# One block and a more detailed timing simulator for the instruction order of a two-layer attention and Mish kernel

## The chip, the cores and the metric

One core of one Trainium2 chip. The metric is the device time of one execution in microseconds (us), as the median of several runs. The core has a matrix engine (TensorE, "PE" in the profile; its weight loads are listed as "PEld"), a vector engine (VectorE, DVE), an activation engine (ScalarE, ACT), a general engine (GpSimd, POOL) and a queue engine (SyncE, SP). Each engine takes its own instructions in the order in which they stand in the program. In this kernel every DMA is issued by SP.

## The reference

Two layers of the same pair of blocks, with the same weights, on x of 2048 rows by 640 columns in float32 (the heads' reshapes are left out):

```
for _ in range(2):
    n = layernorm(x)
    q, k, v = split(n @ wqkv)                 # 32 heads of 20
    pq, pk = q @ w_phi, k @ w_phi             # per head
    phi_q = [softmax(pq), softmax(-pq)]       # 40 features per head
    phi_k = [softmax(pk), softmax(-pk)]
    kv, z = phi_k^T v, sum over rows of phi_k
    x = x + ((phi_q kv) / (phi_q z + 1e-6)) @ wo
    n = layernorm(x)
    x = x + mish(n @ w1 + b1) @ w2            # 640 -> 1536 -> 640
```

## The kernel before

**Precision.** Every product of two activations or weights in the projections and dense layers is made from a high and a low half of each operand: three matmuls (high·high, low·high, high·low). The high half is an ACT copy to a rounded type (`r1h`, `r2h`, `xth`), the low half a subtraction (`r1l`, `r2l`, `xtl`) on DVE or POOL. Weights are split in `split` (L139 to L146): a DMA into a stage `st`, an ACT copy (L145), a subtraction (L146).

**Stages of a layer.** The main loop stands in L1016 to L1043 and calls three functions per layer.

- `attend_first` (L492) goes through 8 blocks of 256 rows, each of two tiles of 128 rows. For each tile it makes a query, a key and a value tile: `project` (L424) runs 30 matmuls of 128 x 320 columns for one. `features` (L459) makes the two softmaxes: ACT copies from PSUM and takes the exponential; DVE reduces (L467, L476) and takes the reciprocal (L477); POOL multiplies (L478) and, for queries, subtracts (L468). For a key tile, 22 small matmuls (L543) add phi_k^T v into two PSUM tiles. Query features are stored to DRAM in `e_d` (L552). Row statistics come from `norm_stats` (L275, L277, DVE) and `norm_scale` (L284, L285 on POOL, L287 on DVE).
- Layer 0 has a start of its own: the query and key weights are loaded raw (L239), centered (L247, L248 on DVE, L249 on ACT), and folded with w_phi on PE (`fold_phi`, L261), then split on ACT and DVE (L266, L267). The value weights come by `load_v_weights` through stages named `st` and `v` (DMA L144). L305 transposes normalized rows, L313 makes their low halves. L514 and L518 store a transposed copy of x.
- `finish_kv` (L621) masks and transposes the accumulated kv (L626 DVE, L633 PE) into `kvb`. It lies inside the turn from `attend_first` to `attend_second`.
- `attend_second` (L640) goes through the blocks again. `load(b)` brings the two `e` tiles back (L650). `features_t` transposes them on PE (L664) and evicts by DVE (L668) or ACT (L670); `averages` runs the small matmuls (L685) and divides on DVE (L694 to L698); `output` multiplies by wo (L713) and adds x (L715). At the end of each block `at(b)` loads and splits a part of w1 or w2, and from b=1 on runs the stages of the dense part's layernorm (`NormColumns`: squares L368 on ACT, centering L363 and sums of squares L373 on DVE, sums over features L360 on PE).
- `dense` (L787) goes through 4 groups of 512 rows and 12 tiles of 128 hidden features: 15 matmuls of `hidden` (L804, 128 x 512), Mish (L763 to L785: exponential on ACT, three DVE steps, logarithm and exponential on ACT, three DVE steps, copy L784 on ACT and subtraction L785 on POOL), and 15 matmuls of `contract` (L817). At its end in layer 0 it begins the next layer: `fetch_first` (L855) loads the first 256 rows of the new x from `x2r_d` (L859), a copy that `turn` (L828, L832) stored, and query weights that layer 0 had put away in `wp_d` (L178).

**Buffers.** Four `big` buffers of 128 x 1280 hold `e` tiles and Mish temporaries, two `x` buffers rows, six `ol` buffers pairs, ten `xt` buffers split rows, four `row` buffers small rows. PSUM has two `mm` tiles of two banks and four `one` tiles of one bank.

**What sets the order.** The kernel is written against a tile framework. It traces the instructions, tracks which buffers each reads and writes, chooses the order of the instructions on each engine, and adds the semaphore waits. `dense` contains `with tc.manual_schedule(engines=...)` (L962): for PE, DVE, ACT and POOL, the order inside it is the written one, from a list of due places (`plan`, `do`); SP is not in the set. In the rest of the kernel the framework chooses, save for some hints: `issue_after` (ACT's copies through `act`, L126 to L133, are chained; `features_t` waits for the last `averages`; `at(b)` for a load). A DMA uses one of eight landing semaphores, so SP, before it issues a DMA, also waits for the landing of the one eight before it.

Of the kernel before, what the change touches and what calls it, by code (L numbers as in the profile page):

```python
# [16 lines left out]
P = 128  # L17
S = 2048
D = 640
F = 1536  # L20
H = 32
DH = 20
KD = D // P
# [14 lines left out]
LAYERS = 2  # L38
# [6 lines left out]
def kernel(  # L45
# [13 lines left out]
    nc = tc.nc  # L59
# [17 lines left out]
    def x_tile():  # L77

        return work.tile([P, KD, SB], F32, tag="x", name="xt", bufs=2)
# [7 lines left out]
    def part_tile(name):  # L87

        return work.tile([P, 2, BLK], F32R, tag="xt", name=name, bufs=10)

    def row_tile(width=D, dtype=F32, name="row"):
        return work.tile([P, VW], dtype, tag="row", name=name, bufs=4)[:, :width]
# [4 lines left out]
    def col_block(t, c0, n):  # L97

        return t.rearrange("(k p) s -> p k s", p=P)[:, :, c0:c0 + n]
# [4 lines left out]
    b1s = const.tile([P, KF], F32, name="b1s")  # L104
# [14 lines left out]
    x0_d = dram.tile([D, S], F32, name="x0_d")  # L119
    x1_d = dram.tile([D, S], F32, name="x1_d")  # L120
    x2_d = dram.tile([D, S], F32, name="x2_d")
# [4 lines left out]
    def act(*args, **kw):  # L126

        if last_act[0] is None:
            ins = nc.scalar.activation(*args, **kw)
        else:  # L130
            with tc.issue_after(last_act[0]):
                ins = nc.scalar.activation(*args, **kw)  # L132
        last_act[0] = ins.ins  # L133
# [5 lines left out]
    def split(hi, lo, src, width, eng, stage=None):  # L139
        for c0 in range(0, width, D):  # L140
            c1 = min(width, c0 + D)
            st = row_tile(name="st") if stage is None else stage()
            st = st[:, :c1 - c0]
            nc.sync.dma_start(st, src[:, c0:c1])  # L144
            nc.scalar.activation(hi[:, c0:c1], st, AF.Copy)  # L145
            eng.tensor_tensor(lo[:, c0:c1], st, hi[:, c0:c1].bitcast(F32), op=ALU.subtract)  # L146

    def r1_pair(k):
        return tuple(wts.tile([P, F], F32R, tag=f"r1{s}{k}", name=f"r1{s}{k}") for s in "hl")
# [4 lines left out]
    def r2_pair(j):  # L154
        if j >= 10:
            w = r2_wide(j)
            return w[:, 0], w[:, 1]
        return tuple(wts.tile([P, D], F32R, tag=f"r2{s}{j}", name=f"r2{s}{j}") for s in "hl")
# [62 lines left out]
    def load_w2(fs):  # L221

        ws = {}
        for f in fs:
            ws[f] = r2_pair(f)
            split(ws[f][0], ws[f][1], w2[f * P:(f + 1) * P, :], D, nc.gpsimd)
        return ws
# [188 lines left out]
    def split_chunk(xt, k, into):  # L416

        hi, lo = (part_tile(n).rearrange("p c s -> p (c s)") for n in ("xth", "xtl"))
        act(hi, xt[:, k], AF.Copy)
        nc.vector.tensor_tensor(lo, xt[:, k], hi.bitcast(F32), op=ALU.subtract)  # L420
        into.append((hi, lo))
# [65 lines left out]
    def fetch_super(src, sb):  # L487
        xt = x_tile()
        nc.sync.dma_start(xt, col_block(src, sb * SB, SB))
        return xt  # L490
# [130 lines left out]
    def finish_kv(kva, kvz, mask):  # L621
# [7 lines left out]
        for src, q0, n in ((acc, 0, 4), (acz, 4, 2)):  # L629
# [6 lines left out]
            else:  # L636
                nc.vector.tensor_copy(kvb[:, 4 * P:5 * P], ps[:120, 0])
                nc.vector.tensor_copy(kvb[:80, 5 * P:5 * P + 42], ps[:80, 1, :42])

    def attend_second(x_src, x_dst, acc, at, at_end):  # L640
        kva, kvz, o_ws, advance = acc
        mask = row_tile(name="mask")
# [82 lines left out]
        for b in range(NB):  # L725
            cur = nxt
            if b + 2 < NB:
                gate = load(b + 2)
            xt = fetch_cols(x_src, b, r2_wide(10 + b % 2, F32).rearrange("p s d -> p (s d)"))
            if b + 1 < NB:  # L730
                with tc.issue_after(num[0]):
                    phs = features_t(b + 1)
                if b == 0:
                    cur.all()
                nxt = averages(phs)
            output(cur, xt, 0)
            if b + 1 < NB:
                nxt.all()
            else:
                for k in range(2):  # L740
                    at_end(k)
            output(cur, xt, 1)
            output(cur, xt, 2)
            if b + 1 == NB:
                for k in range(2, KD):
                    at_end(k)
            nc.sync.dma_start(col_block(x_dst, b * BLK, BLK), xt)
            if b + 1 < NB:
                with tc.issue_after(gate.ins):
                    at(b)  # L750
# [262 lines left out]
        rows, xts, q_ws = begun[0]  # L1013
        return rows, xts, kv_ws, q_ws

    first = None  # L1016
    for layer in range(LAYERS):
        last = layer == LAYERS - 1
        acc = attend_first(layer, x, first)
        if layer == 0:  # L1020
            nc.sync.dma_start(b1s, b1)
        w1s = []
        w2s = {}
        x1t = [None, None]

        def at(b):
            if b < KD:
                w1s.append(r1_pair(b))
                split(w1s[b][0], w1s[b][1], w1[b * P:(b + 1) * P, :], F, nc.gpsimd)
            else:  # L1030
                w2s.update(load_w2(((0, 1), (2, 3, 4))[b - KD]))
            if b == 1:
                x1t[0] = fetch_super(x1_d, 0)
                x1t[1] = NormColumns(x1t[0]).stages()
            elif b in (2, 3, 4):
                next(x1t[1])

        def at_end(k):
            split_chunk(x1t[0], k, first)

        first = []
        attend_second(x2_d if layer else x0_d, x1_d, acc, at, at_end)
        first = dense(x1_d, out if last else x2_d, w1s, w2s, first, last)  # L1043


# [36 lines left out]
```

## Time and profile before

| | |
|---|---|
| runs shown | 1509.74, 1512.21, 1507.96 us; median 1509.74 |
| profiled execution | 1507.05 us, span 1505.2 us, mean granted PE clock 0.995 |
| PE busy / share | 1455.5 us, 97% |
| DVE, ACT, POOL busy | 1157.1, 619.6, 486.1 us |
| PE idle before its first matmul | 9.58 us |
| DMA | 167.89 MB, mean 112 GB/s |

The stages lie about so in the span: `attend_first` from 0 to 280 and 770 to 1010 us, `attend_second` from 280 to 405 and 1010 to 1130, `dense` from 405 to 770 and 1130 to 1505.

How to read the views: a timeline row has the start in us, the duration (of a whole run of like instructions, if the count behind the x is over 1), the engine, the line of the kernel, the operation, output<-inputs, shapes, the count, and in brackets the idle time of the engine just before, with what ended it. A row of the view by windows has the window in us and its length, then the busy time of PE, PEld, DVE, ACT and POOL with the number of instructions, the mean granted PE clock (1.0 is full speed), the share of time in which the DMA engines were busy, and what they moved in GB/s.

### The profile page before, as it was taken

How to read it: one execution, taken by the hardware profiler on the slowest of the kernel's cores; microseconds unless marked ns; L12 is line 12 of the kernel's file. 1: busy time of each engine (PE TensorE's matmuls, PEld its weight loads, DVE VectorE, ACT ScalarE, POOL GpSimd, SP SyncE). 2: the span in 40 equal slices, each digit the busy share in tenths (PEclk: the TensorE clock that was granted, in tenths of full speed). 3: DMA queues.
4: the chain of work that ended last, by engine and by line, in shares of the span. 5: the costliest groups of instructions: out<-in, count | busy, mean ns of one | idle time of the engine just before them, and what ended most of it. 6: DMA issues, size and time to landing. Idle time of an engine off the chain costs nothing. (4 is left out here: it accounts for less than half of the span.)

```text
span 1505.2 us, 24718 instructions
## 1 busy us (share of the span) xinstructions
PE 1455.5 (97%) x9898; PEld 1286.8 (85%) x9898; DVE 1157.1 (77%) x1781; ACT 619.6 (41%) x990; POOL 486.1 (32%) x338
## 2 busy tenths in 40 slices
PE   7999999999999999999999999999999999999998
PEld 6999999898977777777889999989998777777786
DVE  6878878655578898997769877764665889989876
ACT  5534444433254444443333343433325444434433
POOL 0255665432252131221223555442224312212121
PEclk9999999999999999999999999999999999999999
DMA  7364342766420213123375323136754010212111
GB/s 210 105 224 110 123 132 86 262 232 218 153 79 0 71 20 86 49 56 119 74 283 148 127 82 106 45 127 237 257 181 140 1 35 15 56 36 45 61 21 50
DMA packets 190836, 167.89 MB, mean 112 GB/s; under 512 B 120969, under 2 KB 147849, under 8 KB 190721
## 3 DMA queue, kind: packets, MB, share of 16 engines
q1 hardware_dynamic: 190721, 166.31, 35.2%
q8 instruction: 77, 1.26, 0.3%
q14 instruction: 38, 0.31, 0.1%
HBM read 104.02 MB, written 62.26 MB: 110 GB/s over the span
## 5 line engine op out<-in xcount | busy, mean ns | idle before, releaser
L785 POOL TENSOR_TENSOR ol<-big,ol 128x512 fp32r<-128x512 f32 (+1 forms) x98 | 133.9, 1366 | 545.6 <-ACT ol L784 448.5
L817 PE MATMUL mm<-ol,r2h 128*128 128x512 f32 x640 | 214.3, 395 | 4.7 <-ACT ol L784 4.7
L804 PE MATMUL one<-xtl,r1h 128*128 128x512 f32 x480 | 191.2, 398 | 5.2 <-DVE xtl L420 4.4
L804 PE MATMUL one<-xth,r1l 128*128 128x512 f32 x480 | 190.7, 397 | 0.0
L804 PE MATMUL one<-xth,r1h 128*128 128x512 f32 x480 | 190.0, 396 | 0.0
L437 PE MATMUL mm<-r1h,xth 128*128 128x320 f32 x496 | 156.2, 315 | 0.6 <-ACT r L132 0.6
L437 PE MATMUL mm<-r1h,xtl 128*128 128x320 f32 x496 | 153.2, 309 | 0.0
L437 PE MATMUL mm<-r1l,xth 128*128 128x320 f32 x496 | 153.2, 309 | 0.0
L817 PEld LDWEIGHTS mm<-ol,r2h 128*128 128x128 f32 x640 | 120.1, 188 | 36.1 <-ACT ol L784 7.1
L773 ACT ACTIVATE big<-big,two 128x512 f32<-128x512 f32 (+1 forms) x98 | 70.0, 715 | 177.0 <-DVE big L768 177.0
L784 ACT ACTIVATE ol<-big 128x512 fp32r<-128x512 f32 (+1 forms) x98 | 61.1, 623 | 196.5 <-DVE big L780 196.5
L817 PE MATMUL mm<-ol,r2l 128*128 128x512 f32 x320 | 126.6, 396 | 0.0
L804 PEld LDWEIGHTS one<-xtl,r1h 128*128 128x128 f32 x480 | 90.3, 188 | 32.1 <-DVE xtl L420 10.5
L767 DVE TENSOR_SCALAR big<-big 128x512 f32<-128x512 f32 (+1 forms) x98 | 71.9, 733 | 53.9 <-ACT big L763 52.6
L478 POOL TENSOR_TENSOR r<-r,r 128x1280 f32<-128x1280 f32 x32 | 75.7, 2367 | 111.1 <-DVE r L477 107.0
L804 PEld LDWEIGHTS one<-xth,r1l 128*128 128x128 f32 x480 | 90.5, 189 | 21.6
L804 PEld LDWEIGHTS one<-xth,r1h 128*128 128x128 f32 x480 | 90.6, 189 | 21.1
L778 DVE SCALAR_TENSOR_TENSOR one<-big 128x512 f32<-128x512 f32 (+1 forms) x98 | 69.8, 712 | 45.1 <-ACT big L774 38.7
L478 POOL TENSOR_TENSOR big<-big,r 128x1280 f32<-128x1280 f32 x32 | 77.8, 2431 | 72.1 <-DVE r L477 50.3
L437 PEld LDWEIGHTS mm<-r1h,xth 128*128 128x128 f32 x496 | 93.2, 188 | 2.9 <-ACT r L132 0.9
L713 PE MATMUL one<-xth,r2h 128*128 128x256 f32 x320 | 93.2, 291 | 0.6 <-DVE r L715 0.6
L437 PEld LDWEIGHTS mm<-r1l,xth 128*128 128x128 f32 x496 | 93.3, 188 | 0.0
(200 smaller groups left out, 3764.0 us busy)
## 6 DMA issues: line engine op xcount, KB each, us to landing
e_d<-r SPq DMA_DIRECT2D x32, 640.0 KB, 3.5
big<-e_d SPq DMA_DIRECT2D x32, 640.0 KB, 5.5
xt<-x_d SPq DMA_DIRECT2D x16, 1280.0 KB, 6.6
st<-in_w SPq DMA_DIRECT2D x44, 320.0 KB, 3.6
r<-x_d SPq DMA_DIRECT2D x16, 640.0 KB, 4.6
x_d<-r SPq DMA_DIRECT2D x16, 640.0 KB, 3.5
xt<-in_x SPq DMA_DIRECT2D x8, 640.0 KB, 5.8
x_d<-xt SPq DMA_DIRECT2D x64, 80.0 KB, 2.1
```

The lines of the kernel that those rows point to most:

```text
L437: nc.tensor.matmul(ps[c][:, :HC], l[:, sl], r, start=(n == 0), stop=(n == 3 * KD - 1))
L478: nc.gpsimd.tensor_tensor(eg, eg, r.unsqueeze(2).to_broadcast([P, 2 * H, DH]), op=ALU.mult)
L713: nc.tensor.matmul(ps[:, j, :], l, r, start=(i == 0), stop=(i == 3 * KD - 1))
L767: nc.vector.tensor_scalar_min(e, e, E_CAP)
L773: nc.scalar.activation(r, n, AF.Ln, bias=two)
L778: nc.vector.scalar_tensor_tensor(m, n, 2.0, r, op0=ALU.add, op1=ALU.mult)
L784: nc.scalar.activation(ah, n, AF.Copy)
L785: nc.gpsimd.tensor_tensor(al, n, ah.bitcast(F32), op=ALU.subtract)
L804: nc.tensor.matmul(ph, l, r, start=(n == 0), stop=(n == 3 * KD - 1))
L817: nc.tensor.matmul(accs[sb][k][:, c:c + w], l, r[:, c:c + w], start=(f == 0 and n == 0), stop=(f == KF - 1 and n == 2), skip_group_check=True)
```

## The change

The main loop is put into one block that the framework is told to schedule with a timeline simulation; nothing else is edited. In the new program, `dense` keeps its `manual_schedule`. The lines from L1016 on are one higher.

```diff
-    first = None
-    for layer in range(LAYERS):
-        last = layer == LAYERS - 1
-        acc = attend_first(layer, x, first)
...
-        first = []
-        attend_second(x2_d if layer else x0_d, x1_d, acc, at, at_end)
-        first = dense(x1_d, out if last else x2_d, w1s, w2s, first, last)
+    with tc.block(schedule_with_timeline_sim=True):
+        first = None
+        for layer in range(LAYERS):
+            last = layer == LAYERS - 1
+            acc = attend_first(layer, x, first)
...
+            first = []
+            attend_second(x2_d if layer else x0_d, x1_d, acc, at, at_end)
+            first = dense(x1_d, out if last else x2_d, w1s, w2s, first, last)
```

What it does to the instructions: both programs have the same 12,392 matmuls, vector, activation and DMA instructions with the same operands. The new one has one more branch on each engine (into the block), one more load of POOL's library, and about 1308 in place of 1271 separate waits on semaphores. The order differs for 1247 of 8782 matmuls on PE, 471 of 1781 instructions on DVE, 146 of 990 on ACT, 98 of 341 on POOL and 155 of 498 DMAs on SP (by up to 54 places). Inside `dense` the order on PE, DVE, ACT and POOL is the same, except that at the end of layer 0 the row statistics of the next layer's first block (L275, L277, L287 on DVE) stand further ahead. The second layer's dense part is unchanged.

More of the change, by code (lines that the diff above doesn't have):

```diff
@@ L1014, in dense, with at, at_end @@
         return rows, xts, kv_ws, q_ws
-    first = None
-    for layer in range(LAYERS):
-        last = layer == LAYERS - 1
-        acc = attend_first(layer, x, first)
[L1020 to L1039, printed above, removed]
-        first = []
-        attend_second(x2_d if layer else x0_d, x1_d, acc, at, at_end)
-        first = dense(x1_d, out if last else x2_d, w1s, w2s, first, last)
+    with tc.block(schedule_with_timeline_sim=True):
[3 more added lines that the diff above has]
+            acc = attend_first(layer, x, first)
+            if layer == 0:
+                nc.sync.dma_start(b1s, b1)
+            w1s = []
+            w2s = {}
+            x1t = [None, None]
+            def at(b):
+                if b < KD:
+                    w1s.append(r1_pair(b))
+                    split(w1s[b][0], w1s[b][1], w1[b * P:(b + 1) * P, :], F, nc.gpsimd)
+                else:
+                    w2s.update(load_w2(((0, 1), (2, 3, 4))[b - KD]))
+                if b == 1:
+                    x1t[0] = fetch_super(x1_d, 0)
+                    x1t[1] = NormColumns(x1t[0]).stages()
+                elif b in (2, 3, 4):
+                    next(x1t[1])
+            def at_end(k):
+                split_chunk(x1t[0], k, first)
+            first = []
+            attend_second(x2_d if layer else x0_d, x1_d, acc, at, at_end)
+            first = dense(x1_d, out if last else x2_d, w1s, w2s, first, last)
 def kernel(A_x, A_wqkv, A_w_phi, A_wo, B_x, B_w1, B_b1, B_w2):
```

## The prediction

> **What bounds the kernel now.** I read the first two parts of the page first: how busy each engine is, and where in the span.
>
> ```profile
> PE 1455.5 (97%) x9898; PEld 1286.8 (85%) x9898; DVE 1157.1 (77%) x1781; ACT 619.6 (41%) x990; POOL 486.1 (32%) x338
> ...
> PE   7999999999999999999999999999999999999998
> PEclk9999999999999999999999999999999999999999
> ```
>
> TensorE (PE) computes 97% of the span, in all 40 slices. No matmul is removed, so a new order can win only what PE loses now: 1505.2 − 1455.5 = 49.7 us of idle time, and the stretches in which its clock is halved. 9.6 us of the idle time are the wait for the first weights and about 20 us lie in the dense stages, whose order stays. Some 20 us are left to win. Next the timeline of PE, for its gaps outside the dense stages (the largest):
>
> ```profile
> 353.93 0.66 PE L664 MATMUL one<-ident,big 128*120 128x128 f32 x4 [1.20 <-ACT ol L670]
> ...
> 355.97 1.11 PE L664 MATMUL one<-ident,big 128*120 128x128 f32 x4 [0.77 <-ACT ol L670]
> ```
> ```profile
> 1017.65 3.76 PE L664 MATMUL one<-ident,big 128*120 128x128 f32 x18 [3.46 <-DMA big<-e_d]
> ```
>
> In brackets stands how long PE stood idle before the row, and for what. At each of them I asked the busy time by windows of 3.4 us, with the granted clock:
>
> ```profile
> 352.50:355.90 3.40, 1.50 (x23) 0.96 (x20) 2.34 (x5) 2.93 (x7) 1.25 (x2) 0.99 0.58 194
> 355.90:359.30 3.40, 3.33 (x23) 2.39 (x24) 3.18 (x6) 2.09 (x5) 0.00 (x0) 0.50 0.66 205
> ...
> 1014.60:1018.00 3.40, 0.34 (x3) 0.35 (x4) 0.89 (x2) 0.00 (x0) 0.00 (x0) 1.00 0.95 381
> 1018.00:1021.40 3.40, 3.40 (x18) 3.35 (x17) 0.69 (x1) 2.11 (x4) 0.00 (x0) 0.51 0.97 401
> 1082.90:1086.30 3.40, 1.89 (x26) 1.34 (x24) 2.40 (x5) 2.59 (x6) 0.86 (x2) 1.00 0.62 210
> ```
>
> Second column: PE busy; third from the right: clock. Behind a window busy for 1.50 us of 3.40 the clock was 0.50 (6.8 us long at 355.9), behind one of 1.89 it stayed 1.00. So a gap costs itself, and if more than about half of its window is idle, also 1.7 us (3.4 us at half speed) or 3.4 us (6.8 us).
>
> [...]
>
> **The change part by part.** PE's order moves in 1247 of 8782 matmuls, DVE's in 471 of 1781 instructions, SP's in 155 of 498; those of the dense parts stay, but for one place (part 4). Most moves swap independent matmuls of neighbouring tiles in stretches where PE has no gap; these cost nothing while PE is fed, and a matmul moved back is covered by the one that moved up. Six places are left.
>
> **1. Start of layer 0: loss.** SP issues the DMAs in order. Now it is
>
> ```profile
> 6.40 0.33 SPq L239 DMA_DIRECT2D raw<-in_wqk_t  x1
> 7.65 1.61 SPq L144 DMA_DIRECT2D st<-in_wv  x2
> 15.73 0.80 SPq L144 DMA_DIRECT2D v<-in_wv  x2
> 16.59 1.78 SPq L239 DMA_DIRECT2D raw<-in_wqk_t  x4
> ```
>
> In the new order the four key loads of L239 (307 KB each) and the last (102 KB), 1.33 MB, stand ahead of the two `st` and two `v` loads of wv. The windows from 10 to 20 us moved 251 to 295 GB/s with the DMA engines 88% to 101% busy, so 1.33 MB take 4.9 us at 270. The `v` weights landed at 18.7 and 19.6, so about 26 now. PE begins the first value tile at 20.30; the new order runs the first four value tiles' matmuls (60 at 0.147 us) in one piece when the last of these weights is split (L146, 0.82 us each on DVE, behind the key reductions, 0.82 each). By hand that ends near 34.3 with the first query tile still to come: a lag of 4 us at q0, 3 to 3.2 behind k0; the half-empty windows between 21 and 30 may halve the clock for 1 to 2 us more. The floor is 3 (lag only), the ceiling 9 (lag 5 and two halvings of 1.7 to 2). I take 4.5.
>
> **2. Block entry.** One more branch per engine and a library load on POOL. In before, the branch into the kernel lies between 0.33 and 0.71 us: 0.3 to 0.4; bounds 0 and 2 (an instruction fetch from the nearest DMA row, 2 us). I take 0.3.
>
> **3. Block b=5 of attend_second: gain.** In both gaps PE waits for ACT's evictions at L670:
>
> ```profile
> 353.29 0.58 ACT L670 ACTIVATE ol<-one 120x512 f32<-120x512 f32 x1
> 353.77 1.66 ACT L368 ACTIVATE sq<-xt 128x512 f32<-128x512 f32 x3
> 355.33 0.58 ACT L670 ACTIVATE ol<-one 120x512 f32<-120x512 f32 x1
> ```
>
> The squares stand between two evictions; the new order puts them behind, so the second eviction ends 1.66 us earlier and the 0.77 gap goes. The first gap stays (ACT waits for `st` till 352.97). The window is then busy for about 2.2 us, above the 1.89 that kept full clock: the 6.8 us at 0.50 go, worth 3.4. Gain 4.2 (0.8 without the clock); in layer 1, where the clock was kept, 0.8. On DVE the evictions of L668 move ahead of the sums of squares (L373) too; these are wanted one block (15 us) later.
>
> **4. End of layer 0's dense part: a new wait.** The next layer's row statistics (L275 x4 of 0.44, L277) move on DVE ahead of the second to last Mish:
>
> ```profile
> 751.30 0.57 DVE L767 TENSOR_SCALAR big<-big 128x512 f32<-128x512 f32 x1 [1.79 <-ACT big L763]
> ...
> 762.93 0.49 DVE L275 BATCH_NORM_STATS2 bn<-xt 128x6 f32<-128x320 f32 x1 [1.15 <-DMA xt<-x2r_d]
> ```
>
> They wait for rows loaded by L859. Before, SP issued it at 755.75, behind two weight loads that waited till 754.70, and it landed at 762.8. In the new order L859 stands ahead of these, so it can go when the last store of x2r_d has landed (748.3, from stores issued till 745.8). The same load took 3.7 to 4.8 us alone (826.50→830.37, 857.91→862.69): landing 752.9 to 754.8 with 0.7 us of issue. Four L275 and two L277 (2.1 us) follow, and behind them on DVE stands the whole Mish: it starts at 755.5 to 756.8 in place of 751.30, 4.2 to 5.5 late. ACT's next rows (L763 of the last Mish) queue behind it. POOL's L785 of this Mish ended at 758.36 and PE wanted it at 760.81, so 2.4 us are covered. The last Mish starts some 4.5 late, but wins back the 1.5 us that L275 and L277 stood between its halves (763.34 in place of 761.8) and 0.9 that the last L780 waited for L287: its last eviction (767.31) comes 2.1 later. Of these PE fills 1.1 (its gaps of 0.85 and 0.31 there) with the first query matmuls, which the new order mixes in. Net −1 (bounds +0.6 and −4); each later microsecond of landing costs one.
>
> **5. Turn of layer 1 from attend_first to attend_second: gain.** In the trace load(1) of `e_d` left at 1010.68 and 1011.72, behind the store of the last `e` at 1011.21, and PE waited 3.46 us, followed by 3.4 us at half clock (1.7). The new order runs the last two kv groups in one piece, so their `big` buffers come free sooner, and puts the load ahead of the store. By the issue-to-landing row of this load (5.5 us) the gap shrinks to 1.0–1.3 and the window stays over half busy: gain 2.6 + 1.7 = 4.3, bounds 0.5 and 5.2. At layer 0's turn (gap 1.32) the store stays ahead; gain 0.5, with a risk that the 2 us of gaps there come together.
>
> **6. kv of tile 32** (PE waits 1.06 us at 810.01 for POOL's L478): it moves behind a value tile of 4.4 us: gain 1.06. The dense gaps stay, but the windows of the clock shift against them: at 1178.4 PE was busy for 1.14 of 3.4 and lost 1.7, at 451.5 for 2.10 and lost nothing; either can turn, ±1.7, taken as 0.
>
> **Sum** against the profiled run (1507.05: span 1505.2 and 1.85 around it): gains 4.2 + 0.8 + 4.3 + 0.5 + 1.06 = 10.9; losses 4.5 + 0.3 + 1.0, and 0.8 for a halving at a new place (half of 1.7) = 6.6. Net −4.3: 1502.8. This run lies 2.7 under the median of the runs shown, so as a median **1505.5**.
>
> **The rivals.**
> - **A, all halvings go and the start is cheap** (lag 2, part 4 costs nothing): 1507.05 − 10.9 + 2.3 = 1498.5, as a median 1501; with the dense halving of 1181.8 gone too (1.7) and part 5 at its bound (0.9) 1498.5. For it: PE has 5 us of fold and transposes to do meanwhile. Against: 1.33 MB do stand in front.
> - **B, slower: the rows at part 4 land no earlier than before.** The stores of x2r_d are many small pieces, and the profile gives no landing for the last. If the landing stays at 762.8, the Mish starts at 765, 13.6 us late; by the same steps (−2.4 −1.1) PE loses 10 us in place of 1, and 1.7 to 3.4 of half clock behind the gap: 1505.5 + 9 + 2.5 = 1517. It turns slower than 1514.3 from a landing near 760, 6 us behind the 753.8 I take. Against: the two loads that held L859 up are behind it now.
> - **C, slower: the start costs 9 and part 5's gain fails to come** (the e_d load, in a stream 95% busy at 381 GB/s, still lands late): 1505.5 + 4.5 + 4.3 = 1514.5.
> - **D, nothing that can be measured:** order moves where PE is full, the half clock at 355.9 stays though the gap goes, and start and turn cancel: 1505.5 + 3.4 = 1508.9, 1507.5 to 1510.5.
>
> **How the numbers follow.** Forecast 0.50, A 0.13, D 0.13, B 0.14, C 0.10. The forecast's own range is 1500 to 1510. About 0.3% (4.5 us) is what a measurement of this kernel can tell from no change. Below 1505.2: A and 0.27 of the forecast, 0.40. Within: D and 0.23, 0.36. Above 1514.3: B and C, 0.24. The range 1497 to 1518 leaves out the ends of A, B and C.
>
> **What would show it.** PE idle between 20 and 34 us (part 1: the first query tile 3 to 5 us later); clock 1.0 at 350–365 and at 1010–1022; one gap in place of two at L664 in b=5; on DVE the wait before L275 near 750 and its length: 3 to 5 us as taken, 12 in B. The forecast is wrong if moved matmuls open gaps inside the steady blocks of attend_first (30–270, 775–1005), where I found no wait at risk.

## The result, and the profile after

The median of four runs is 1516.97 us (1515.83 to 1518.10); the kernel before, run beside it, has 1508.85 (four runs). The ratio is 1.005, with a 95% interval of 1.0031 to 1.007: the change costs 8.1 us, 0.5%. The time lies within the range of the prediction, but on the other side of no change from the forecast of 1505.5.

The profiled execution took 1517.54 us with a span of 1515.7, against 1507.05 and 1505.2: 10.5 us more in the span. The busy line of the page after:

```profile
PE 1461.8 (96%) x9898; PEld 1288.7 (85%) x9898; DVE 1167.4 (77%) x1781; ACT 620.1 (41%) x990; POOL 486.8 (32%) x338
```

PE is busy for 6.3 us longer with the same matmuls, and idle for 1515.7 − 1461.8 = 53.9 us in place of 49.7. The change closed some gaps and opened others.

Half clock explains little of the longer busy time: between its first rise and 1500 us the clock was at half for 17.0 us in place of 13.6, worth 1.7. Most of the rest lies in attend_second at full clock: in blocks 1 to 4 PE is busy for 2.7 us longer in layer 0 (281 to 352 us before, 286.1 to 359.4 after) and 2.2 in layer 1 (1024 to 1079, 1028.0 to 1086.2).

Both programs have the same matmuls, so I set the end of each group of them (a projection, an eviction's transposes, a block's output) in one trace beside its end in the other; the difference is the lag of the kernel after. By stage, with what the prediction had for it:

| stage (us, before) | lag at its end | change in the stage | predicted |
|---|---|---|---|
| start, to about 100 | 6.7 | +6.7 | +4.8 |
| rest of attend_first, turn of layer 0 | 4.3 | −2.4 | −0.5 |
| layer 0, attend_second, blocks 1 to 4 | 7.4 | +3.1 | 0 |
| block b=5 | 3.65 | −3.75 | −4.2 |
| blocks 6 and 7 | 5.4 | +1.7 | 0 |
| dense of layer 0 | 5.55 | +0.2 | 0 |
| end of layer 0 | 4.6 | −1.0 | +1.0 |
| attend_first of layer 1 | 5.4 | +0.8 | −1.06 |
| turn of layer 1 | 4.7 | −0.7 | −4.3 |
| layer 1, attend_second, blocks 1 to 4 | 7.2 | +2.5 | 0 |
| block b=5 | 6.4 | −0.9 | −0.8 |
| blocks 6 and 7 | 8.15 | +1.8 | 0 |
| dense of layer 1 and the end | 10.5 | +2.35 | 0 |

The rows of PE after that answer to the gaps shown before, from its timeline (start, duration, tile; in brackets the idle time ahead):

```profile
10.62 1.21 PE L261 MATMUL mm<-big,raw 120*128 120x120 f32 x4 [10.62 <-ACT raw L249]
...
22.99 0.41 PE L437 MATMUL one<-r1h,xth 128*128 128x320 f32 x1 [1.63 <-ACT r1h L145]
...
342.30 0.65 PE L664 MATMUL one<-ident,big 128*120 128x128 f32 x4 [0.89 <-DVE r L715]
...
361.11 0.65 PE L664 MATMUL one<-ident,big 128*120 128x128 f32 x4 [0.98 <-ACT ol L670]
...
388.02 0.53 PE L305 MATMUL one<-ident,o 128*128 128x128 f32 x3 [1.44 <-DVE o L698]
...
836.03 0.41 PE L437 MATMUL mm<-r1h,xthl 128*128 128x320 f32 x1 [1.65 <-DVE xthl L313]
...
1021.02 3.93 PE L664 MATMUL one<-ident,big 128*120 128x128 f32 x19 [1.96 <-DMA big<-e_d]
```

(Line numbers in the text are those of the kernel before; in rows of the experiments' kernels a line can stand a few places lower.) In b=5 there is one gap (361.11) where there were two, as forecast. The gap at the turn of layer 1 is 1.96 us, not 3.46. But the waits at 342.30 and 388.02, for DVE, stand in blocks where before had 0.57 at most, and 836.03 is new too.

One loss shows no gap at all. In a block of attend_second without a wait, PE's timeline was (first fence) and is (second):

```profile
1050.79 2.56 PE L664 MATMUL one<-ident,big 128*120 128x128 f32 x22
1053.29 2.77 PE L685 MATMUL mm<-kvb,ol 120*64 120x63 f32 x88
```
```profile
1055.75 2.34 PE L664 MATMUL one<-ident,big 128*120 128x128 f32 x20
1058.03 0.68 PE L685 MATMUL mm<-kvb,ol 120*64 120x63 f32 x16
1058.64 0.41 PE L664 MATMUL one<-ident,big 128*80 128x128 f32 x2
1058.98 2.35 PE L685 MATMUL mm<-kvb,ol 120*64 120x63 f32 x72
```

The new order puts the last two of the 22 transposes among the 88 averages. From the first start to the last end the same 110 matmuls took 5.27 us and take 5.58, with no idle time and a full clock. Three other blocks that wait for nothing (those at 390.5, 1035.4 and 1118.4 in before) show the same 0.3 us. Twelve blocks have two transposes among the averages after and not before; at 0.32 each that would be 3.8 us, an estimate.

The clock, by windows of 3.4 us (columns as in the prediction):

```profile
21.40:24.80 3.40, 1.27 (x5) 0.78 (x6) 2.05 (x5) 2.54 (x6) 0.00 (x0) 0.99 1.07 368
24.80:28.20 3.40, 3.40 (x12) 2.95 (x13) 3.40 (x10) 3.40 (x8) 0.00 (x0) 0.50 1.05 208
...
1018.10:1021.50 3.40, 1.44 (x31) 1.20 (x26) 2.47 (x8) 0.00 (x0) 0.00 (x0) 0.99 1.01 410
1021.50:1024.90 3.40, 3.40 (x19) 3.06 (x17) 0.69 (x1) 1.79 (x3) 0.00 (x0) 0.50 0.85 263
```

From 28.2 to 458.3 the clock is full, so the 6.8 us of half clock in b=5 are gone. There are 3.4 new us of it at the start (24.8 to 28.2) and in the first dense part (458.3 to 461.7), 3.4 at the turn of layer 1 as before, and 6.8 in place of 3.4 in the second dense part (1188.7 to 1195.5).

SP's rows of the places that the prediction priced:

```profile
6.33 5.31 SPq L239 DMA_DIRECT2D raw<-in_wqk_t  x5
...
19.52 1.93 SPq L144 DMA_DIRECT2D v<-in_wv  x2
```
```profile
1013.25 2.83 SPq L650 DMA_DIRECT2D big<-e_d  x3
```

The key loads all stand ahead of the last four loads of wv; the two `v` loads among these left from 19.52 on, behind a row load and a store too, and landed at 25.67 and 26.52. At the turn, the store of an `e` tile (1012.41) is still ahead of the second load of `e_d`, which left when the last kv group had ended (1013.22).

### The profile page after: what moved, and what is told of

Same layout as the page of the kernel before. It is cut to its first block, busy times and chain, and to the rows that moved or that the text cites. A ratio compares the mean times of both kernels' runs of the same rounds, so it can differ in the third digit from the quotient of the medians.

```text
span 1515.7 us, 24758 instructions
## 1 busy us (share of the span) xinstructions
PE 1461.8 (96%) x9898; PEld 1288.7 (85%) x9898; DVE 1167.4 (77%) x1781; ACT 620.1 (41%) x990; POOL 486.8 (32%) x338
## 5 line engine op out<-in xcount | busy, mean ns | idle before, releaser
L478 POOL TENSOR_TENSOR r<-r,r 128x1280 f32<-128x1280 f32 x32 | 76.4, 2387 | 109.3 <-DVE r L477 105.4
L478 POOL TENSOR_TENSOR big<-big,r 128x1280 f32<-128x1280 f32 x32 | 79.5, 2485 | 56.9 <-DVE r L477 35.5
L713 PE MATMUL one<-xth,r2h 128*128 128x256 f32 x320 | 93.1, 291 | 1.6 <-DVE r L715 1.6
L437 PEld LDWEIGHTS mm<-r1h,xtl 128*128 128x128 f32 x496 | 93.2, 188 | 0.3 <-DVE xtl L313 0.2
```

The costliest lines, as they stand in the source:

```text
L437: nc.tensor.matmul(ps[c][:, :HC], l[:, sl], r, start=(n == 0), stop=(n == 3 * KD - 1))
L478: nc.gpsimd.tensor_tensor(eg, eg, r.unsqueeze(2).to_broadcast([P, 2 * H, DH]), op=ALU.mult)
L713: nc.tensor.matmul(ps[:, j, :], l, r, start=(i == 0), stop=(i == 3 * KD - 1))
```

## The experiments

Each ratio is to the kernel before, run beside it; the interval is at 95%. Lags are those of one profiled execution. My theory after the result was that the loss is made in two places: at the start, and by an order in attend_second in which DVE's work for another stage stands ahead of what PE waits for. The rivals were the mere fact of a block, the detailed simulator's choice as such, and the clock.

### The block without the simulator

`e1_plain_block` puts the same block around the loop but leaves the simulation out; few instructions move (88 matmuls, 59 on DVE, 29 DMAs, all near the start).

```diff
+    with tc.block():
```

> The same block without the timeline simulation: the order of before returns but for places near the start (88 matmuls, 59 DVE instructions, 29 DMAs differ from before). Theory (the loss lies in the order that the detailed simulator chose, place by place): within 3 us of before, and attend_second without the gaps at 341 and 386 us. Rival (the block itself costs: its entry, or what the scheduler no longer sees across its edge): 5 to 9 us slower than before, like the changed kernel.

Measured: 1513.94 us, ratio 1.0047 (1.003 to 1.0064). This was a surprise: a loss nearly as large. In the profiled execution, the slowest of the five, 8.75 of the 10.1 us of lag were made by 50 us; from there on the trace runs nearly parallel to that of before. Two stretches of PE's timeline show where (plain block):

```profile
17.12 0.65 PE L261 MATMUL mm<-big,r 40*128 40x40 f32 x2
...
33.43 0.47 PE L437 MATMUL one<-r1l,xth 128*128 128x320 f32 x1
33.70 0.41 PE L437 MATMUL one<-r1h,xtl 128*128 128x320 f32 x1
33.95 0.31 PE L437 MATMUL one<-r1l,xth 128*128 128x320 f32 x1
34.09 0.31 PE L437 MATMUL one<-r1h,xtl 128*128 128x320 f32 x1
```

Up to 33.9 the starts of these matmuls lie 0.267 us apart, behind it 0.147: the clock was at half until then. (The clock column shows 1.00 ahead of a trace's first change; the spacing tells the rate there: in the kernel after the same matmuls lie 0.267 us apart from 24.8 to 28.2, where the column shows 0.50, and 0.147 behind.) In before it rose at 14.5: its L261 pairs on `big,r` take 0.41 us from 16.24 on, these 0.65. Yet PE was busy for 84% to 100% of each window from 10 to 30 us.

### The start: the order of the loads

`e2_before_keys_first` is the kernel before with the key loads put ahead of four of the five loads of wv; `e3_after_loads_pinned` the kernel after with the key loads and the next row load held behind them.

```diff
-            nc.sync.dma_start(st, src[:, c0:c1])
+            with tc.issue_after(raw_loads[-1]) if src.tensor is wv.tensor and 1 <= len(loads) <= 4 else nullcontext():
+                loads.append(nc.sync.dma_start(st, src[:, c0:c1]).ins)
```

> Before, without a block, with the key loads of the start issued ahead of four of the five value-weight loads, nothing else pinned. Theory (part 1: the loads' order sets the start): 4 to 7 us slower than before, all of it by 60 us, the same lag from there to the end. Rival (PE's order, value tiles in one piece, is what costs): within 2 us of before, since PE can still mix query and fold matmuls in.

> The changed kernel with the key loads, all but the first, and the next block's row load pinned behind the value-weight loads. Theory: 4 to 6.5 us faster than the changed kernel, so 2 to 4 us slower than before; the losses in attend_second stay. Rival 1 (all later losses follow from the shifted start): as fast as before or faster. Rival 2 (PE's order at the start, not the loads): within 2 us of the changed kernel.

Measured: 1509.13 us, 1.0016 (1.0003 to 1.0029) for the first, whose trace lags by 0.1 to 0.7 us up to 1010; 1514.02, 1.0046 (1.003 to 1.0062) for the second, whose lag behind the start is 3.5 in place of 6.7, in a profile that is the fastest of its five runs; by the median it is not shown to be faster than the kernel after. So the key loads ahead alone cost little, against my part 1: the framework then gave PE another order at the start. Late weights cost with PE's order that waits for them (22.99 in the rows of after: PE stands 1.63 us, and the window of 21.4 is a third busy). Two things are not apart in this pair: in `e2` the `v` loads left from 15.91 on, 3.6 us ahead of those of after, and in `e3` PE's order at the start changed with the loads.

### The start alone under the simulator

`e9_sim_first_only` puts only layer 0's attend_first into the simulated block.

```diff
+        with tc.block(schedule_with_timeline_sim=True) if not layer else nullcontext():
```

> The simulated block around attend_first of layer 0 alone, all behind it outside of the block in before's way. Theory (the start is the largest single loss of the changed kernel, by gaps of PE and the half clock behind them): PE 5 to 8 us behind before at 60 us, the same lag up to the end, 4 to 8 us slower than before. Rival (the start's loss is given back where the kernel waits later anyway): within 2 us of before.

Measured: 1518.51, 1.0081 (1.006 to 1.0102). The order of PE, DVE and ACT at the start is that of the kernel after, and the lag is 6.4 us from 100 to 270: the start's loss, alone, confirmed. Behind the end of the block the `e_d` loads leave late (283.85; the first two left from 266.37 on in before), PE waits 5.74 us for one at 288.82, and the lag grows by 4.8, with 6.8 us at half clock. From 300 on, in before's order, the lag lies between 8.8 and 11.8. In the first three blocks of layer 1's attend_second it stays at 9.47, where that of the kernel after grows from 4.63 to 5.29 without a gap: the transposes among the averages come with the simulated order.

### Warming the clock

Six dummy matmuls of 512 columns at the very start, in the kernel before (`e5_before_warm`) and in the plain block (`e6_plain_block_warm`); they compute nothing that is used.

```diff
+    heat = one_tile()
+    for _ in range(6):
+        nc.tensor.matmul(heat.rearrange("p (c s) -> p c s", c=4), ident,
+                         ident.unsqueeze(1).to_broadcast([P, 4, P]), start=True, stop=True)
```

> Before, with six extra matmuls of the identity by itself (512 columns each, result read by nobody) put at the start, where PE waits 9.6 us for the first weights. [...]

> The plain block of the first run with the same six extra matmuls. New theory (the plain block lost 8.7 us because PE ran at half clock till 33.9): the clock rises before the first fold, the whole loss goes: 7 to 11 us faster than the plain block, from 4 us faster than before to 1 slower. Rival (entry into the block or its order costs): no more than 3 us faster than the plain block.

Measured: 1518.92, 1.0073 (1.0056 to 1.009), and 1511.31, 1.0033 (1.0018 to 1.0048). In the plain block's profiled run the clock was full from 7.6 to 355.7 us, the lag behind the start 0.7, and the span 1507.2, 8.1 less than without. But its order at the start had changed too, so the clock is not shown to be the whole of that. The medians differ by only 2.6, which is what the rival said, and the runs spread (1507.4 to 1518.7). In the kernel before, the framework changed the order as well, and PE waited 3.20 us at 11.28; the clock rose, fell, and then stayed at half from 21.0 to 34.7 with PE fully busy (one of the windows of this kernel):

```profile
21.00:24.40 3.40, 3.34 (x13) 3.05 (x14) 2.42 (x7) 2.21 (x7) 0.00 (x0) 0.51 1.06 299
```

Busy for 3.34 of 3.40, and the rate stayed at half for three windows more: being busy in the profile did not lift the clock by itself.

### attend_second: averages, stages, and the row load

`e4_after_averages_apart` holds the second tile's averages behind the first's, as I thought that the new order lost by mixing them. `e7_before_stages_late` and `e8_after_stages_late` write the layernorm stages behind the next block's averages.

```diff
+                        with tc.issue_after(head) if t else nullcontext():
```
```diff
             output(cur, xt, 0)
             if b + 1 < NB:
                 nxt.all()
+                stage(b)
...
-            elif b in (2, 3, 4):
+        def stage(b):
+            if b in (3, 4, 5):
```

> The changed kernel with the second tile's averages pinned behind the first tile's on PE. Theory (mixing the two tiles' averages makes the first tile's division on DVE late, and with it the transposes of L305): the gaps before L305 and L713 in blocks 6 and 7 (1.44 and 0.78) fall to the 0.57 and 0.29 of before, 1.4 us in each layer, and some tenths in each other block: 3 to 5 us faster than the changed kernel. Rival (the averages are covered, the gaps come from the late load of x at L489): within 1 us of the changed kernel.

> Before, with the three layernorm stages of attend_second written behind the next block's averages in place of ahead of its transposes. Theory (ACT's squares ahead of the evictions make the two gaps at 353 us, and the gaps carry the 6.8 us at half clock): ACT evicts first, the gap of 0.77 goes, the half clock at 355 with it, and 0.8 in layer 1: 3.5 to 6 us faster than before. [...]

> The changed kernel with the same edit. Theory (its losses in attend_second come from layernorm work on DVE, L350 and L392, placed ahead of what PE waits for, L715 and L698): the gaps at 341 and 386 us and those of layer 1 go, 4 to 7 us faster than the changed kernel, the start's loss stays. Rival (the mixed averages and the late load of x are the cause): within 2 us of the changed kernel.

Measured: 1525.02, 1.0132 (1.0109 to 1.0155); 1512.75, 1.0039 (1.0027 to 1.0051); 1517.64, 1.0069 (1.0056 to 1.0083). None of the three gave the time of its theory, though in `e7` the gaps and the half clock at 353 went, for some 5 us that it lost again behind. With the two tiles' averages apart, the gaps ahead of L305 in block 6 grew from 1.44 to 2.43 and 3.35, with half clock behind each, so that this mixing is not the loss. (The two transposes among the averages stayed in `e4`; no run takes them out of the kernel after.) With the stages late, four centerings L363 in one piece (2.47 us) stand on DVE ahead of the low halves L313 that L713 reads: PE waits 2.82 us there (364), and 2.54 at 393 for `r` of L715, in the kernel before. In the kernel after it waits 2.21 us at the first of these places and 1.83 for `o` of L698.

What makes the gaps of blocks 4 and 6 is seen on DVE after:

```profile
339.30 0.69 DVE L350 TENSOR_TENSOR s<-xt 128x512 f32<-128x512 f32 x1 [2.63 <-DMA xt<-x_d]
...
341.56 0.68 DVE L715 TENSOR_TENSOR r<-one,r 128x512 f32<-128x512 f32 x1
...
383.08 3.09 DVE L392 TENSOR_TENSOR xt<-xt,rstd 128x512 f32<-128x512 f32 x5
...
386.62 0.69 DVE L715 TENSOR_TENSOR r<-one,r 128x512 f32<-128x512 f32 x1
387.22 0.88 DVE L698 TENSOR_TENSOR o<-mm,den 128x480 f32<-128x480 f32 x2
```

At 336.67 DVE stands still for 2.63 us: the sum over features (L350) waits for a row tile. Its load (L489) left at 329.12 and landed at 339.17, 10.0 us later; before, it left at 323.46 and DVE, after a wait of 0.61, went on 8.2 us later. The kernel after lags by 5.7 us at this place, so the load left no later; but now two loads of `e_d` left just ahead of it (327.91), where it was one before, and it landed some 1.8 us later on PE's clock. Behind L350 in DVE's queue is L715, which frees the PSUM tile that PE wants at 341.41. In block 6 the five scalings L392 stand in one piece ahead of the division L698, and PE waits 1.44 for `o`. This piece of 3.10 us is in before too (379.18), with a wait of 0.57; new is the residual add L715 between it and the first division. `e10_after_fetch_pinned` moves the load back ahead, `e12_after_loads_and_fetch` is this with `e3` together.

```diff
+                with tc.issue_after(last_super[0].ins) if b == 4 and t else nullcontext():
                 ins = nc.sync.dma_start(es[t], e_d[b * BT + t])
```

> The changed kernel with the load of the dense part's first rows (L489) pinned ahead of the two e_d loads that its order puts before it. Theory (this load lands 7 us later than in before, DVE waits for it at L350 ahead of the residual add of L715, and PE for that): the gaps at 341 to 344 and 1072 to 1075 us (1.5 and 1.0 in all) go, 2 to 3.5 us faster than the changed kernel. Rival (e_d then lands late instead, or another wait on DVE takes its place): within 1 us.

> The changed kernel with both the start's loads and the load of L489 pinned. If the two places add up: 5 to 7 us faster than the changed kernel, 1 to 4 slower than before. If they don't (the clock's windows, shifted, take another gap in): as the run with the start's loads pinned, 6 to 8 slower than before.

In `e10` PE's order is that of the kernel after, and the load leaves ahead of both loads of `e_d` (its timeline of SP):

```profile
329.42 0.38 SPq L490 DMA_DIRECT2D xt<-x_d  x1
```

It lands 7.1 us later, and PE's gaps at that place go, but for two of 0.36 and 0.20 at 345.66 and 346.78. The lag made in layer 0's blocks 1 to 4 falls from 3.1 to 1.6 us. In layer 1 the same edit wins nothing: the load leaves at 1060.28, ahead of the `e_d` loads, DVE still waits 2.08 us for it, and blocks 1 to 4 add 2.7 us of lag (2.5 without the edit). The whole takes 1513.34 us, 1.0045 (1.0027 to 1.0063); the kernel after had 1.005, so no gain is shown. `e12` has 1514.09, 1.0042 (1.0028 to 1.0056): the two together give no more than one. Its profiled run shows a reason: PE's order is that of `e3`, yet the clock was at half from 20.4 to 30.7 and the lag 6.2 in place of 3.5. With one order on PE the two profiles differ by 2.7 us.

### The evictions first, written by hand

`e11_before_evict_first` is the one gain that I saw, taken alone into the kernel before: the squares L368, and the weight loads with their splits, behind the next block's evictions.

```diff
+                if b:
+                    with tc.issue_after(gate.ins):
+                        loads(b - 1)
...
+        def stage(b):
+            if b == 4:
+                next(x1t[1])
```

> Before, with only the squares and the weight loads of attend_second written behind the next block's averages; the centering stays where it is, since moving it made PE wait 2.8 us at L713. Theory: both gaps at 353 us (1.97) and the half clock behind them (3.4) go, and 1.9 in layer 1: 4 to 7 us faster than before. Rival (the squares now stand ahead of the splits of L132 that output waits for): no faster, a gap of 1 to 2 us before L713 in block 5.

Measured: 1508.63, 1.0021 (1.0007 to 1.0035). The two gaps at 353 became one of 2.04, and the clock stayed full there. It leads by 2.8 us at 370, and gives them back: a gap of 1.78 at 373, where the weight copies L145 now stand between two evictions and wait 3.15 us for their load, and 5.51 in place of 3.46 at the turn of layer 1, with 6.8 us of half clock.

### Filling gaps, for the clock

Dummy matmuls into a free PSUM tile while PE would be idle, to see whether the half clock goes: at layer 1's turn (`e13_before_fill_turn`, 14 of 0.21 us), there, in b=5 and in the dense gaps (`e14_before_fill_three`), in the first fold of the plain block (`e15_plain_block_fill_fold`, 20), and at four places of the kernel after (`e16_after_fill_four`).

```diff
+    def fill(ps, n):
+        for _ in range(n):
+            nc.tensor.matmul(ps.rearrange("p (c s) -> p c s", c=4), ones,
+                             ones.unsqueeze(1).to_broadcast([P, 4, P]), start=True, stop=True)
```

> Before, with 14 extra matmuls (128x512, result overwritten, 0.21 us each) on PE at layer 1's turn, where it waits 3.5 us for e_d; they do no work of the kernel. [...]

> Before, with such extra matmuls at three places, in PE's waits: the turn of layer 1 (14), block 5 of attend_second in both layers (5 each), the first layernorm sum of each dense part (5 each). Theory: no half clock between 15 and 1490 us; 1.7 + 3.4 + 1.7 less what the fill delays (up to 0.5 a place): 4 to 7 us faster than before, and less scatter between runs. [...]

> The plain block with 4 extra matmuls (128x512) in each of the 5 column groups of the first fold, 20 in all, 4 to 8 us of PE time added. [...]

> The changed kernel with the extra matmuls at the three places of the run before and 8 ahead of the first value tile, where it waits 1.6 us for weights. If its loss is for a good part half clock: 4 to 8 us faster than the changed kernel, 1 to 4 slower than before. If the loss lies in the gaps and the order: within 2 us of the changed kernel.

Measured, in this order: 0.9992 (0.9973 to 1.001); 1.0009 (0.9992 to 1.0027); 1.0045 (1.0029 to 1.0061); 1.0101 (1.0078 to 1.0125). None is shown to win time: the first two intervals hold 1, the plain block alone had 1.0047 and the kernel after 1.005. In `e13` the half clock at the turn goes and the gap is 1.03 (that at 355 goes too, without a fill there), but 6.8 us at half appear at 451 and at 1086. In `e14` PE comes to the turn 2 us earlier, the `e_d` load lands no earlier, and the gap is 3.39 again. In `e15` the clock rises at 6.8, falls at 10.2 behind a gap of 3.44, and stays at half to 27.3. `e16` got another order on DVE and ACT, so that it is no clean test of the clock.

### The scalings spread out

The five L392 scalings are written one at a time behind the steps of block 5's output, in the kernel after (`e17_after_scale_spread`) and before (`e18_before_scale_spread`).

```diff
     output(cur, xt, 0)
+            at_scale(b)
...
+        def at_scale(b):
+            if b == 5:
+                next(x1t[1])
```

> The changed kernel with the five L392 scalings written one at a time behind the steps of block 5's output; in its order on DVE they still stand ahead of the first tile's division (L698), but the residual add (L715) now stands behind it. Nothing else moves on PE or SP. Theory (the gaps of 1.44 and 0.78 in block 6 come from this order on DVE): the 1.44 falls by 0.7, the 0.78 stays; about 0.7 a layer, within 2 us of the changed kernel in all. Rival (the mixed averages are the cause): both gaps as they were.

> Before with the same edit; here two of the five scalings stand between the divisions and the rest behind. Theory: the gaps before L305 and L713 at 383 and 1111 us (0.57 and 0.29) go, 0 to 2 us faster than before. Rival (something else holds L305): the gaps stay, same time.

Measured: 1514.20, 1.0045 (1.0027 to 1.0062), and **1503.88, 0.9975 (0.9958 to 0.9992)**, with 1508.31 for the kernel before beside it. The second beats both kernels. On its DVE the divisions now stand between the scalings, and PE's transposes of `o` (379.32) come without a wait (its timeline of DVE):

```profile
376.82 0.89 DVE L699 TENSOR_TENSOR o<-mm,den 128x480 f32<-128x480 f32 x2
...
377.70 0.68 DVE L392 TENSOR_TENSOR xt<-xt,rstd 128x512 f32<-128x512 f32 x1
```

The idle times of 0.57 and 0.29 ahead of L305 and L713 there are gone; by the groups PE wins 1.0 us in block 6 of each layer, 2 of the 4.4 us. The rest of the profiled run's lead is mostly 2.9 us in b=5, where the gaps stayed (1.22 and 0.78) but the windows that hold them were busy for 2.38 and 2.42 us of 3.40 and the clock stayed at 1.00 (before: 1.50, then 0.50); I take that part for chance in one profile, and the interval, one of eighteen here, allows a gain from 1 to 6 us. In `e17`, where the scalings still stand ahead of the first division but L715 behind it, the gap of 1.44 fell to 0.66: L715's place makes some 0.8 of it.

## Why the prediction was wrong

**The step that failed** is the sentence under "The change part by part": "Most moves swap independent matmuls of neighbouring tiles in stretches where PE has no gap; these cost nothing while PE is fed, and a matmul moved back is covered by the one that moved up." Blocks 1 to 4 and 6 to 7 of attend_second, priced at nothing, cost 3.1 + 1.7 + 2.5 + 1.8 = 9.1 us. The sentence fails in two ways. The swap itself is not free: two transposes among the averages make a block 0.3 us longer on a PE that never waits. And what moved with the matmuls on DVE and SP was not covered: PE waits at 342 for L715, at 388 for L698. I had counted that DVE moves in 471 of 1781 instructions and SP in 155 of 498, and looked only at six places for a wait. The warning that I gave named attend_first, not attend_second. `e10` shows one of these waits by itself (1.5 us of lag in layer 0's blocks 1 to 4 for one load), `e17` another (0.8 for one residual add), `e9` that the blocks' growth without a gap comes with the order; for the rest the place is seen in the rows, not tried one by one. That the time lies inside the range is luck: no rival priced attend_second's blocks, and the rival whose number it meets, B at 1517, rests on rows that land late, which did not happen.

**Part 1, start.** Sign right, size short: 6.7 (6.4 in `e9`) against 4.8 with the block entry; inside the bounds of 3 to 9. The `v` weights landed at 25.67 and 26.52, as forecast (26). The 3.4 us of half clock, for which I had 1 to 2 us as a possibility, are worth 1.7; the six profiles with this order at the start (after, `e4`, `e8`, `e9`, `e10`, `e17`) all have them, or 6.9 us. And the cause was put on the loads alone (`e2`: 0.3 us of lag behind the start).

**Part 2, block entry.** First matmul at 10.62 in place of 9.58, inside the bounds; `e1` (9.49) shows that a block as such costs nothing there.

**Part 3, b=5.** Right: 3.75 for 4.2, 0.86 for 0.8. One gap, clock full.

The half clock went with one of the two gaps: in the kernel after, the windows from 357.0 and 360.4 were busy for 3.13 and 2.69 us of 3.40 and the clock stayed at 1.00, where before had 1.50 and then 0.50.

**Part 4, end of layer 0.** Sign wrong, small: the rows were there at 757.05 on a clock that lags 5.55, so 751.5 in before's time, earlier than the 752.9 to 754.8 taken (the second should be 753.8: 748.3 + 0.7 + 4.8); the stage won 1.0 in place of losing 1.0. DVE's wait was 1.98 us:

```profile
757.08 1.68 DVE L275 BATCH_NORM_STATS2 bn<-xt 128x6 f32<-128x320 f32 x4 [1.98 <-DMA xt<-x2r_d]
```

Rival B, the slower one to which I gave the most, did not happen, though its 1517 is the time measured.

**Part 5, turn of layer 1.** 0.7 for 4.3. "The new order ... puts the load ahead of the store" held for the first tile's load only. The second tile's buffer comes free when the last kv group has ended, and that end moved by only about 1 us (1009.58 before; 1013.22 after, on a clock that lags by 4.7). PE's wait ends with this load: it left at 1013.25 and landed at 1020.97, 7.7 us later, where I took the 5.5 of the profile page's row for all such loads, a median; before, PE went on 7.0 us after the load of 1010.68 had left. With 5.5 it would have landed before PE was free (1019.06). The gap shrank by 1.5, and behind the window that holds most of it, busy for 1.44 of 3.40, the clock was again at 0.50. At layer 0's turn, 2.4 us came in place of 0.5.

**Part 6, kv of tile 32.** The 1.1 us came, and 1.65 at 834 took them back: DVE's L470, one of the steps ahead of L313 there, took 2.98 us beside a step on POOL, where one without took 0.81 (last section). The second dense part and the end cost 2.35 where I took 0 within ±1.7 and set 0.8 aside for a halving anywhere; 1.3 of it come where the clock is at half for 6.8 us in place of 3.4 (near 1190), the rest in steps of 0.3 whose cause I did not look for.

**Sum.** The gains that came are 2.4 + 3.75 + 1.0 + 0.7 + 0.9 = 8.75 us (10.9 forecast); the losses 6.7 + 3.1 + 1.7 + 0.2 + 0.8 + 2.5 + 1.8 + 2.35 = 19.15 (6.6 forecast). By its mechanism rival C (1514.5; its own terms give 1514.3) comes nearest, with half of it right: part 5 failed; but the start cost less than its 9, and the larger loss was in no rival.

**What stays open.** How the start's 6.7 us part into PE's order and the clock: with one and the same order of PE, DVE and ACT the lag behind the start was 5.0 (`e8`), 6.2 (`e17`), 6.4 (`e9`), 6.7 (after, `e4`) and 7.4 us (`e10`), and that of `e3` and `e12` 3.5 and 6.2. What the transposes among the averages cost in all is an estimate. The plain block loses over 7 us in timed runs, but its half clock is seen in one profile, and the dummy matmuls win back less in the median than in the profile. `e3`, `e10`, `e12` and `e17` all stand at 1.0042 to 1.0046 against 1.005 of the kernel after: their intervals overlap its own, so none is shown to be faster than it.

## What to carry to other kernels

When a scheduler reorders a kernel whose main engine is full, don't take a moved matmul for free, even where PE never waits (here 0.3 us a block): set the time of a whole group of them before and after side by side. Then list what moved on each other queue, and for each instruction that now waits earlier or later name what stands behind it. Here a load that went out behind one more load of 640 KB cost 1.5 us of lag (`e10`), and a vector step ahead of the one that PE waited for 0.8 (`e17`), in blocks whose gaps had been 0.57 at most. And a change of under 1% is to be tested on several runs: with one order on PE the lag behind the start was 3.5 us in one profile here and 6.2 in another (`e3`, `e12`).

## What the runs showed of the hardware

**Half clock and PE's busy time.** I cut the traces of before and after into windows of 3.413 us from the rise at 14.53 on; all later changes of the clock fall on their edges. At full clock, half clock came behind seven windows, in which PE was busy for 0.40, 1.23 and 1.54 us (before) and 1.09, 1.24, 1.25 and 1.45 (after); each was idle for more than half, as the prediction took it. Behind all others, busy for 1.76 us or more, the clock stayed full, but for the last one at full clock in each trace (1.93 and 2.39, near the end). At half clock, busy time does not part the windows: the clock rose behind one of 2.97 us and those of 3.41, and stayed at half behind one of 2.80 (after, 1188.71) and one of 3.31 (before, 355.86). Likewise in the plain block: PE was busy for 84% to 100% of each window from 10 us on, and the rise came at 33.9, 19 us later than in before. What decided there is not shown.

**DVE beside POOL.** In after, at the place of the 836.03 gap (timelines of DVE and POOL):

```profile
820.56 0.81 DVE L470 TENSOR_TENSOR r<-m,r 128x640 f32<-128x640 f32 x1
...
827.74 2.98 DVE L470 TENSOR_TENSOR big<-m,big 128x640 f32<-128x640 f32 x1
```
```profile
827.42 2.61 POOL L478 TENSOR_TENSOR big<-big,r 128x1280 f32<-128x1280 f32 x1 [1.43 <-DVE r L477]
```

This DVE step took 0.81 us with no step on POOL, and 2.98 where POOL's multiplication had begun 0.32 us before it: that one ends at 830.03, and DVE's 0.69 us behind. In the traces of before and after, the 92 steps of L470 without a POOL step beside them take 0.78 to 0.83 us. The 20 that began while a step L146, L199 or L478 was running on POOL take 1.48 to 2.99, and each ends 0.68 or 0.69 us behind it. In nine cases (all in after) such a step, or an L195, began on POOL 0.11 us or more behind the start of DVE's: those take 0.76 to 0.83. At the place shown, the longer step stands on DVE ahead of the L313 for which PE waits 1.65 us at 836.03.
